# Half-height transposes, products as the stationary side and a split add in a fused RWKV and soft-MoE kernel

## The chip, the cores and the metric

The kernel runs on one core of one Trainium2 chip. The metric is the device time of one execution in microseconds (us); lower is better. The kernel before took 188.74 us as the median of three executions (191.13, 188.74 and 188.16).

In the profile PE is the matrix engine (TensorE) and PEld its weight loads, DVE the vector engine, ACT the scalar engine, POOL the general one (GpSimd), and SP the engine that issues the DMAs (SyncE). Each runs its own list of instructions in order; one that waits holds up what stands behind it on the same engine.

## The reference

Attention of the RWKV kind is computed for 4 batches, 8 heads, 768 steps and 48 features, then a soft mixture of experts on the 3072 rows that it gives.

```python
def _attn_ref(r, k, v, w, u):
    for t in range(S):
        kt, vt, rt, wt = (k[:, :, t], v[:, :, t], r[:, :, t], w[:, :, t])
        cur = np.einsum('bhd,bhe->bhde', u[None] * kt, vt)
        y[:, :, t] = np.einsum('bhd,bhde->bhe', rt, state + cur)
        state = wt[:, :, :, None] * state + np.einsum('bhd,bhe->bhde', kt, vt)

def _moe_ref(x, phi, w1, w2):           # x: 3072 x 384, 8 experts of 4 slots, F = 1024
    logits = x @ phi
    d = np.exp(logits - logits.max(0, keepdims=True))
    d /= d.sum(0, keepdims=True) + 1e-09
    slot_input = (d.T @ x).reshape(E, S_per_e, D)
    for e in range(E):
        slot_out[e] = np.maximum(slot_input[e] @ w1[e], 0.0) @ w2[e]
    c = np.exp(logits - logits.max(1, keepdims=True))
    c /= c.sum(1, keepdims=True) + 1e-09
    return c @ slot_out.reshape(n_slots, D)
```

## The kernel before, in words

**Tiling.** The 32 heads go in 16 pairs; two heads of 48 features stand on partitions 0 to 47 and 64 to 111. The 768 steps are cut into C = 6 chunks of P = 128. Within a chunk the recurrence is written as matrices. With the decays multiplied into r and k by scans, the scores k x r of a chunk, masked to earlier steps, times v give the part from within the chunk; a state carried between chunks, times r, gives the rest; and the term with u is a number per step, a = sum of u * r * k, times v. Of each batch the first three pairs of heads are loaded with all 128 partitions, whose spare rows (48 to 63 and 112 to 127) hold a third of the fourth pair each; the fourth pair's rows are gathered by DMA into tiles of their own (`k3`, `r3`, `kn3`).

**The loop.** `for it in range(NIT + 1)` is a loop of slots, unrolled, 17 of them. Slot `it` does three things for three different pairs: it prepares pair `it` (decay scans, the number a), computes pair n = it - 1 (scores, state, y), and takes pair m = it - 2 out of PSUM into x and on to the logits. What a slot contains depends on `it % 4`: slots 4, 8, 12 and 16 compute a gathered pair, whose keys need no transpose; slots 3, 7, 11 and 15 prepare no new unit, so have no `d_a`; slots 2, 6, 10 and 14 have no turn of x (`X` is false, as a third of the 384 columns of x isn't yet complete) and, from 6 on, hold steps of the softmax over the batch before.

**The order.** `tc.manual_schedule()` is on: what stands first in the loop's body goes first on each engine, and nothing is reordered. The tiles of the PSUM pool `ps_t` (four buffers), from which nearly all small PE results come, are taken in turn, so that a PE step that takes the next buffer waits for the copy that empties it. `y` has one buffer, `ps_y`.

**The steps that the change and the prediction name**, with the lines of the profile of before:

- keys, or kn: `b_kn` (matmul L298, copies L299 and L302 on ACT): transposes of five chunks of keys
- scores: `b_scores` (L313; ACT copies `at` L317; mask on POOL L318), two halves of three chunks
- `d_a` (L252; ACT copy `aT` L255) and turn of a, `d_a_turn` (L260; ACT copy `a` L263): sum over features of u * r * k, with u as the stationary operand, and its transposes. r * k is made by POOL in `d_rk` (L244)
- `b_u` (L329): keys x v for each chunk; `b_state`: the state scan `Sb` on DVE (L335) and its copy `Sn` on ACT (L338)
- x turn: `l_turn` (L384; ACT copies `xT` L386); logits, `l_part` (L401; DVE addition `lt` L410)
- `c_av` (L350): masked scores x v into y; `c_inter` (L365): r x state into the same y
- `d_av` (L284, POOL): av = v * a; `c_evac` (L375, DVE): x = y + av
- decay scans on DVE (L206 to L220), by the plans FIRST and SECOND, about half of them ahead of the state scan and half behind it; `a_pat` or `spread` (L224, ACT): the pattern for the state scan
- fillers: `keep_warm` (L793), matmuls on zeros whose result isn't used; before, only in the first two slots

## Time and profile before

| | us |
|---|---|
| median of 3 executions | 188.74 |
| the profiled execution | 189.19 |
| its span, first to last instruction | 187.4 |
| PE busy in it | 165.8 (88%) |
| DVE busy | 121.5 (65%) |
| ACT busy | 90.8 (48%) |
| POOL busy | 76.5 (41%) |
| slot 9 (76.66 to 84.19) | 7.53 |
| slot 10 (84.19 to 91.23) | 7.04 |
| slots done, start of the tail (135.2) | to 187.4: 52.2 |

Busy times of a whole span mix the loop, where DVE runs nearly all the time, with the tail of experts, where it has little to do; what a step in the loop is worth is read in a slot. In the rows of a timeline the first number is the start in us from the span's start, the second the time from the first instruction's start to the last one's end, then engine, line, operation, what it writes and reads, shapes and how many; in brackets how long the engine had been idle before and what released it. On PE the end of an instruction overlaps the start of the next, so the cost of a step there is the distance between starts. A matmul of 32-bit numbers leaves two records, a transpose one. "issue" as a releaser means that the engine waited for nothing that the profile shows.

### The profile page before, as it was taken

How to read it: one execution, taken by the hardware profiler on the slowest of the kernel's cores; microseconds unless marked ns; L12 is line 12 of the kernel's file. 1: busy time of each engine (PE TensorE's matmuls, PEld its weight loads, DVE VectorE, ACT ScalarE, POOL GpSimd, SP SyncE). 2: the span in 40 equal slices, each digit the busy share in tenths (PEclk: the TensorE clock that was granted, in tenths of full speed). 3: DMA queues.
4: the chain of work that ended last, by engine and by line, in shares of the span. 5: the costliest groups of instructions: out<-in, count | busy, mean ns of one | idle time of the engine just before them, and what ended most of it. 6: DMA issues, size and time to landing. Idle time of an engine off the chain costs nothing.

```text
span 187.4 us, 7253 instructions
## 1 busy us (share of the span) xinstructions
PE 165.8 (88%) x3000; PEld 116.6 (62%) x3000; DVE 121.5 (65%) x237; ACT 90.8 (48%) x266; POOL 76.5 (41%) x133
## 2 busy tenths in 40 slices
PE   7499979799999889999899999899789999999710
PEld 2166758677878758688777787787554324755510
DVE  5599978867897977989799889731335222033520
ACT  3054547455677726667765586784450002022430
POOL 3357286572448567445577643557004000000000
PEclk9999999969999999999999999999999999999985
DMA  5999599995779999389999259497999159907692
GB/s 148 339 396 358 116 388 328 357 406 193 230 224 366 323 397 346 75 238 319 299 368 390 53 169 285 117 330 249 418 320 415 73 167 415 417 17 294 261 385 94
DMA packets 14249, 51.93 MB, mean 277 GB/s; under 512 B 2304, under 2 KB 3200, under 8 KB 13568
## 3 DMA queue, kind: packets, MB, share of 16 engines
q1 hardware_dynamic: 14208, 51.38, 77.3%
q8 instruction: 26, 0.43, 0.9%
q14 instruction: 15, 0.12, 0.2%
HBM read 44.28 MB, written 4.72 MB: 261 GB/s over the span
## 4 chain that ended last, share of the span: by engine, by line
PE 48%; DVE 27%; DMA 7%; ACT 7%; issue 5%; POOL 1%; SPq 0%; ACTq 0%; DVEq 0%; POOLq 0%
PE ap L313 9%; DVE cst L218 6%; PE hp L536 6%; PE so L572 6%; DVE cst L206 5%; DMA rt<-in_wkr_dram 5%; PE y L365 5%; DVE Sb L335 4%; DVE ld L217 3%; PE tp L384 3%; PE op L601 3%; PE up L329 3%; ACT Sn L338 3%; PE tp L298 3%; PE sp L448 3%
## 5 line engine op out<-in xcount | busy, mean ns | idle before, releaser
L318 POOL TENSOR_SCALAR_AFFINE_SELECT at<-at 128x384 f32<-128x384 f32 x64 | 31.2, 523 | 28.7 <-ACT at L317 28.7
L317 ACT COPY at<-ap 128x384 f32<-128x384 f32 x64 | 26.4, 490 | 6.8 <-PE ap L313 5.6
L350 PE MATMUL y<-vt,at 128*64 128x48 f32 x768 | 25.5, 223 | 0.0
L350 PEld LDWEIGHTS y<-vt,at 128*64 128x64 f32 x768 | 23.7, 138 | 2.3 <-POOL at L318 1.7
L284 POOL TENSOR_TENSOR av<-vt,a 128x576 f32<-128x576 f32 x16 | 18.5, 1154 | 13.7 <-ACT a L263 13.7
L218 DVE TENSOR_TENSOR_SCAN cst<-ld,cst 128x387 f32<-128x387 f32 x24 | 23.2, 968 | 0.8
L313 PE MATMUL ap<-rt,ld 48*128 48x128 f32 x288 | 22.8, 286 | 0.7 <-issue 0.7
L206 DVE TENSOR_TENSOR_SCAN cst<-ld,cst 128x387 f32<-128x387 f32 x24 | 22.9, 953 | 0.8 <-DMA ld<-in_wkr_dram 0.6
L244 POOL TENSOR_TENSOR rk<-rt,ld 128x384 f32<-128x384 f32 x24 | 20.3, 868 | 7.3 <-DMA rt<-in_wkr_dram 4.1
L313 PEld LDWEIGHTS ap<-rt,ld 48*128 48x128 f32 x288 | 20.1, 187 | 2.2 <-issue 1.3
L335 DVE TENSOR_TENSOR_SCAN Sb<-up,pat 112x288 f32<-112x288 f32 x16 | 12.1, 753 | 11.9 <-ACT pat L224 7.4
L375 DVE TENSOR_TENSOR x<-y,av 128x576 f32<-128x576 f32 x16 | 12.1, 756 | 8.9 <-PE y L365 8.9
L338 ACT COPY Sn<-Sb 112x240 f32<-112x240 f32 x16 | 10.1, 629 | 12.2 <-DVE Sb L335 12.2
L386 ACT COPY xT<-tp 128x384 f32<-128x384 f32 x24 | 10.3, 482 | 9.0 <-PE tp L384 9.0
L217 DVE TENSOR_TENSOR ld<-ld,cst 128x387 f32<-128x387 f32 x24 | 13.0, 542 | 2.2 <-POOL rk L244 2.2
L365 PE MATMUL y<-Sn,rt 48*64 48x48 f32 x480 | 10.1, 222 | 4.6 <-ACT Sn L338 2.7
L365 PEld LDWEIGHTS y<-Sn,rt 48*64 48x64 f32 x480 | 8.4, 134 | 9.4 <-issue 3.6
L299 ACT COPY kn<-tp 128x336 f32<-128x336 f32 (+1 forms) x24 | 9.6, 401 | 8.9 <-PE tp L298 8.7
L220 DVE TENSOR_TENSOR rt<-rt,cst 128x387 f32<-128x387 f32 x24 | 13.4, 558 | 0.8
L329 PEld LDWEIGHTS up<-vt,kn 128*48 128x48 f32 x320 | 8.8, 128 | 7.0 <-issue 5.8
L572 PE MATMUL so<-wt,hT 128*32 128x208 f32 (+1 forms) x256 | 12.5, 329 | 0.0
L384 PE MATMUL tp<-ident,x 128*128 128x128 f32 x72 | 10.9, 289 | 1.0 <-DVE x L375 1.0
(130 smaller groups left out, 241.9 us busy)
## 6 DMA issues: line engine op xcount, KB each, us to landing
wt<-in_w_dram SPq DMA_DIRECT2D x24, 512.0 KB, 7.1
ld<-in_wkr_dram SPq DMA_DIRECT2D x11, 775.0 KB, 6.4
wt<-in_w_dram SPq DMA_DIRECT2D x5, 1536.0 KB, 9.0
vt<-in_v_dram SPq DMA_DIRECT2D x16, 288.0 KB, 4.9
rt<-in_wkr_dram SPq DMA_DIRECT2D x11, 387.0 KB, 5.9
wt<-in_w_dram SPq DMA_DIRECT2D x3, 832.0 KB, 6.4
out_dram<-wt SPq DMA_DIRECT2D x3, 832.0 KB, 3.9
wt<-in_w_dram SPq DMA_DIRECT2D x3, 704.0 KB, 10.1
```

Of the source, the lines that this page charges most:

```text
L206: nc.vector.tensor_tensor_scan(out=prod[:, ::-1], data0=t[:, lo + 1:lo + 1 + HALF * E1][:, ::-1], data1=one, initial=1.0, op0=ALU.mult, op ...
L217: nc.vector.tensor_tensor(out=k_, in0=k_, in1=prod, op=ALU.mult)
L218: nc.vector.tensor_tensor_scan(out=prod, data0=lds[i % NL][:, lo:lo + HALF * E1], data1=big, initial=1.0, op0=ALU.mult, op1=ALU.min)
L244: nc.gpsimd.tensor_tensor(out=rks[i % 2].rearrange("p (c e) -> p c e", e=P)[:, part], in0=queries(i)[:, part], in1=keys(i)[:, part], op=AL ...
L284: nc.gpsimd.tensor_tensor(out=av, in0=st["vv"], in1=a.broadcast_to([P, 2, C, D]), op=ALU.mult)
L313: nc.tensor.matmul(out=aps[h][:, cc, :], lhsT=kt_[rows, c * E1 + 1:(c + 1) * E1], rhs=rt_[rows, c * E1:c * E1 + P], start=True, stop=True)
L317: nc.scalar.copy(out=at, in_=aps[h])
L318: nc.gpsimd.affine_select(out=at, in_=at, pattern=[[0, 3], [1, P]], compare_op=ALU.is_gt, fill=0.0, base=0, channel_multiplier=-1)
L335: nc.vector.tensor_tensor_scan(out=Sb[0:ROWS].rearrange("p e n -> p (e n)"), data0=up[0:ROWS].rearrange("p e n -> p (e n)"), data1=(pat3 i ...
L350: nc.tensor.matmul(out=st["y"][cols, h, c * D:(c + 1) * D], lhsT=st["AT", h, hf][:, cc, cols], rhs=st["vv"][:, h, c, :], start=(c == 0), s ...
L365: nc.tensor.matmul(out=st["y"][cols, h, c * D:(c + 1) * D], lhsT=t[rows, c * E1 + 64 * th:c * E1 + 64 * th + 64], rhs=Sn[rows, c - 1, :], ...
L572: nc.tensor.matmul(out=so[32 * g:32 * g + NS, :], lhsT=hT[ft // 2][:, ft % 2, e, :], rhs=wts[E + e][:, base + ft * wd:base + (ft + 1) * wd ...
```

## The change

1. `d_a` makes r * k the stationary side, in 12 pieces of 64 steps, and moves four columns of u past each. The result has the steps on the partitions at once, so that `d_a_turn` and the copy `aT` are gone; one copy `a` on ACT is left.
2. The transposes of keys and of x are made in half-height pieces of 64 rows, which lie in two row tiles of PE: ten matmuls for five, twelve for six. The two PSUM tiles of a turn now hold the two halves by rows, not by chunks. ACT makes as many copies, cut otherwise.
3. `c_evac`, for all pairs but the last: DVE adds av to the first head of y, ACT copies the second head's y from PSUM into x, and POOL adds av to it there.
4. The order of a slot: `c_evac` first; then the scores; `d_a`; the keys' turn; `d_av`; the turn of x; and `b_u` behind it. Before: `d_av`, keys, first half of the scores, `c_evac`, second half, `d_a`, `b_u`, turn of x.
5. Fillers before `c_inter` in slots 2, 3 and 4 (six each), 8 and 12 (two each), 16 (three).

On PE, slots 9 and 10 before (`ld_99`, `ld_100`: decayed keys; `rt_103`, `rt_104`: queries):

```order
L298 MATMUL tp<-ident,ld_99 128x128 x5
L313 MATMUL ap<-rt_103,ld_99 128x128 x12
L252 MATMUL aps<-rk_134,u_sb 32x256 x3
L329 MATMUL up<-vt,kn 48x48 x10
L384 MATMUL tp<-ident,x 128x128 x6
L350 MATMUL y<-vt,at 64x48 x24
L260 MATMUL atp<-ident,aT 128x96 x2
L401 MATMUL lp<-xT,phi_sb 32x256 x3
L365 MATMUL y<-Sn,rt_103 64x48 x20
L298 MATMUL tp<-ident,ld_100 128x128 x5
L313 MATMUL ap<-rt_104,ld_100 128x128 x12
L252 MATMUL aps<-rk_133,u_sb 32x256 x3
```

and the same slots after (the steps have new lines: scores L308, `d_a` L254, keys L294, x turn L387, `b_u` L324, `c_av` L345, logits L403, `c_inter` L360):

```order
L308 MATMUL ap<-rt_103,ld_99 128x128 x12
L254 MATMUL aps<-u_sb,rk_134 64x4 x12
L294 MATMUL tp<-ident,ld_99 128x64 x10
L387 MATMUL tp<-ident,x 128x64 x12
L324 MATMUL up<-vt,kn 48x48 x10
L345 MATMUL y<-vt,at 64x48 x24
L403 MATMUL lp<-xT,phi_sb 32x256 x3
L360 MATMUL y<-Sn,rt_103 64x48 x20
L308 MATMUL ap<-rt_104,ld_100 128x128 x12
L254 MATMUL aps<-u_sb,rk_133 64x4 x12
L294 MATMUL tp<-ident,ld_100 128x64 x10
```

The scores moved ahead of the keys' turn, and `b_u` moved behind the turns of keys and of x; the two transposes of a are gone.

On ACT, slot 10 before (`kn_139` is the gathered pair's tile of keys):

```order
L299 COPY kn<-tp 128x336
L302 COPY kn_139<-tp 128x3x2x16
L299 COPY kn<-tp 128x224
L302 COPY kn_139<-tp 128x2x2x16
L317 COPY at<-ap 128x384 x4
L255 COPY aT<-aps 96x256
```

and after:

```order
L377 COPY x<-y 128x6x48
L312 COPY at<-ap 128x384 x4
L258 COPY a<-aps 128x6x4
L296 COPY kn<-tp 128x5x48 x2
L298 COPY kn_139<-tp 128x5x16 x2
```

The copy of y into x now stands ahead of the four copies of scores, and the kn copies behind them. With its waits its row reads

```order
L377 COPY x<-y 128x6x48 [waits DVE_49]
```

in each of the 15 slots; the DVE instruction that it waits for is L376, the addition for the other head of the same tile x.

The diff:

```diff
--- before.py
+++ after.py
@@ -26,6 +26,7 @@
 END_TOL = 1e-4
 N_WARM = 16
 N_WARM_2 = (5, 3, 5, 8)
+N_WAIT = {2: 6, 3: 6, 4: 6, 8: 2, 12: 2, 16: 3}
 N_FILL = (4, 3)
 N_WA = 8
 N_WB = 3
@@ -43,6 +44,7 @@
 
 NL = 4
 PART = 16
+HP = P // 2
 
 HALF = 3
 
@@ -246,22 +248,14 @@
 
     def d_a(i):
 
-        ap = ps_t.tile([TG, 2, P], F32, name="aps", tag="tp")
-        rkc = rks[i % 2].rearrange("p (c e) -> p c e", e=P)
-        for j in range(NTG):
-            nc.tensor.matmul(out=ap[32 * j:32 * j + 32], lhsT=u_sb[:, i % NU, :], rhs=rkc[:, j:C:NTG, :],
-                             start=True, stop=True)
-        parts[i] = aT = small.tile([TG, 2, P], F32, name="aT", bufs=1)
-        nc.scalar.copy(out=aT, in_=ap)
-
-    def d_a_turn(i):
-        tp = ps_t.tile([P, 2, P], F32, name="atp", tag="tp")
-        for n in range(2):
-            nc.tensor.transpose(out=tp[:, n, 0:TG], in_=parts[i][:, n, :], identity=ident[0:TG, 0:TG])
-
+        ap = ps_t.tile([P, C, 4], F32, name="aps", tag="tp")
+        for c in range(C):
+            for th in range(2):
+                nc.tensor.matmul(out=ap[HP * th:HP * th + HP, c, :],
+                                 lhsT=rks[i % 2][:, c * P + HP * th:c * P + HP * th + HP],
+                                 rhs=u_sb[:, i % NU, 0:4], start=True, stop=True)
         parts[i] = a = small.tile([P, 4, C, 1], F32, name="a", bufs=5)
-        nc.scalar.copy(out=a.rearrange("p h (n j) o -> p h n (j o)", n=2),
-                       in_=tp[:, :, 0:TG].rearrange("p n (j q) -> p q n j", q=32)[:, 0:4])
+        nc.scalar.copy(out=a.rearrange("p h c o -> p c (h o)"), in_=ap)
 
     def d_a_last(b):
         a3[b] = t = small.tile([P, 2, C, 1], F32, name="a3")
@@ -283,24 +277,25 @@
         a = a3[i // NG] if i % NG == NU else parts[unit(i)][:, 0:2]
         nc.gpsimd.tensor_tensor(out=av, in0=st["vv"], in1=a.broadcast_to([P, 2, C, D]), op=ALU.mult)
 
-    def b_kn(i, hf):
+    def b_kn(i, lo, hi):
         st = sts[i]
         if i % NG == NU:
             st["kn"] = kn3
             return
-        if hf == 0:
+        if lo == 0:
             st["kn"] = once.tile([P, C - 1, ROWS], F32, name="kn")
         kn, kv = st["kn"], keys(unit(i))
         at3 = PART * (i % NG)
-        lo, hi = ((0, 3), (3, C - 1))[hf]
-        tp = ps_t.tile([P, 3, P], F32, name="tp")
+
+        tps = [ps_t.tile([P, hi - lo, HP], F32, name="tp") for _ in range(2)]
         for c in range(lo, hi):
-            nc.tensor.transpose(out=tp[:, c - lo, :], in_=kv[:, c, :], identity=ident)
-        nc.scalar.copy(out=kn[:, lo:hi, :], in_=tp[:, 0:hi - lo, 0:ROWS])
-        src = tp[:, 0:hi - lo, :].rearrange("p c (h q) -> p c h q", h=2)[:, :, :, D:64]
-        dst = kn3[:, lo:hi, :]
-        nc.scalar.copy(out=bass.AP(tensor=dst.tensor, offset=dst.offset + at3,
-                                   ap=[dst.ap[0], dst.ap[1], [64, 2], [1, PART]]), in_=src)
+            for h in range(2):
+                rows = slice(HP * h, HP * h + HP)
+                nc.tensor.transpose(out=tps[h][:, c - lo, :], in_=kv[rows, c, :], identity=ident[rows, rows])
+        for h in range(2):
+            nc.scalar.copy(out=kn[:, lo:hi, 64 * h:64 * h + D], in_=tps[h][:, :, 0:D])
+        for h in range(2):
+            nc.scalar.copy(out=kn3[:, lo:hi, 64 * h + at3:64 * h + at3 + PART], in_=tps[h][:, :, D:HP])
 
     def b_scores(i, hf):
         st = sts[i]
@@ -372,20 +367,27 @@
         b, g = divmod(i, NG)
         if g == 0:
             xb[b] = xpool.tile([P, C, DM], F32, name="x")
-        nc.vector.tensor_tensor(
-            out=xb[b][:, :, 2 * g * D:(2 * g + 2) * D].rearrange("p c (h d) -> p h c d", h=2),
-            in0=st["y"][:, :, 0:C * D].rearrange("p h (c d) -> p h c d", c=C), in1=st["av"], op=ALU.add)
-
-    def l_turn(x, kt, pool_s, pool_t, fill=None):
+        dst = xb[b][:, :, 2 * g * D:(2 * g + 2) * D].rearrange("p c (h d) -> p h c d", h=2)
+        src = st["y"][:, :, 0:C * D].rearrange("p h (c d) -> p h c d", c=C)
+        if i == NIT - 1:
+            nc.vector.tensor_tensor(out=dst, in0=src, in1=st["av"], op=ALU.add)
+            return
+
+        nc.vector.tensor_tensor(out=dst[:, 0], in0=src[:, 0], in1=st["av"][:, 0], op=ALU.add)
+        nc.scalar.copy(out=dst[:, 1], in_=src[:, 1])
+        nc.gpsimd.tensor_tensor(out=dst[:, 1], in0=dst[:, 1], in1=st["av"][:, 1], op=ALU.add)
+
+    def l_turn(x, kt, pool_s, pool_t):
+
         xT = pool_s.tile([P, C, P], F32, name="xT")
-        for hf in range(2):
-            tp = pool_t.tile([P, 3, P], F32, name="tp")
-            for j in range(3):
-                nc.tensor.transpose(out=tp[:, j, :], in_=x[:, 3 * hf + j, kt * P:(kt + 1) * P],
-                                    identity=ident)
-            nc.scalar.copy(out=xT[:, 3 * hf:3 * hf + 3, :], in_=tp)
-            if fill and hf == 0:
-                fill()
+        tps = [pool_t.tile([P, C, HP], F32, name="tp") for _ in range(2)]
+        for c in range(C):
+            for th in range(2):
+                rows = slice(HP * th, HP * th + HP)
+                nc.tensor.transpose(out=tps[th][:, c, :], in_=x[rows, c, kt * P:(kt + 1) * P],
+                                    identity=ident[rows, rows])
+        for th in range(2):
+            nc.scalar.copy(out=xT[:, :, HP * th:HP * th + HP], in_=tps[th])
         return xT
 
     def l_seed(lt, pool_t, tag):
@@ -857,22 +859,16 @@
             d_rk(0)
             scans(0, (("G", 0), ("F", 0), ("G", 1), ("F", 1)))
             d_a(0)
-            d_a_turn(0)
             keep_warm(N_WARM_2[0], ps_t, "tp")
             d_rk(1)
         if ph == NU:
             d_a_last(it // NG)
+        if m >= 0:
+            c_evac(m)
         if B_:
-            d_av(n)
-            b_kn(n, 0)
-            if n:
-                b_kn(n, 1)
             b_scores(n, 0)
             if not n:
                 keep_warm(N_WARM_2[1], ps_t, "tp")
-                b_kn(n, 1)
-        if m >= 0:
-            c_evac(m)
         if it != 1:
             pieces_of(it, FIRST)
         if B_:
@@ -880,13 +876,16 @@
         if A and it:
             d_a(i)
         if B_:
-            b_u(n)
-        if Y:
-            s_exp(mb - 1, qs[mb - 1])
+            b_kn(n, 0, C - 1)
+            d_av(n)
         if X:
             xT = l_turn(xb[mb], mg - 1, once, ps_t)
             if mg == 1:
                 lts[mb] = small.tile([TG, 2, P], F32, name="lt", bufs=1)
+        if B_:
+            b_u(n)
+        if Y:
+            s_exp(mb - 1, qs[mb - 1])
         if B_:
             if not U_:
                 spread(pat3, k3)
@@ -910,8 +909,6 @@
             c_y(n)
             c_av(n, 0)
             c_av(n, 1)
-        if A and it:
-            d_a_turn(i)
         if X:
             l_part(mg - 1, xT, lts[mb], ps_t)
         if done is not None:
@@ -927,6 +924,8 @@
             s_slots(xb[mb - 1], mb - 1, qs[mb - 1], ps_t)
         if it == 1:
             keep_warm(N_WARM_2[3], ps_t, "tp")
+        else:
+            keep_warm(N_WAIT.get(it, 0), ps_t, "tp")
         if B_:
             c_inter(n, 0)
             c_inter(n, 1)
```

## The prediction

> **What bounds the kernel now.** I read the page first, for the span, the clock and the chain that ended last; then the windows of single slots of the loop; then the timelines of two neighbouring slots, engine by engine. From the page:
>
> ```profile
> span 187.4 us, 7253 instructions
> ...
> PE 48%; DVE 27%; DMA 7%; ACT 7%; issue 5%; POOL 1%; SPq 0%; ACTq 0%; DVEq 0%; POOLq 0%
> ```
>
> TensorE (PE) carries 48% of the chain and the vector engine (DVE) 27%. The profiled run took 189.19 us, so 1.8 us lie around its span of 187.4, and it is 0.45 above the median of 188.74: a sum made against 189.19 is lowered by 0.45 at the end. The change touches the loop only. Slots 9, 10 and 11, whose limits I cut at the first matmul of each (after length: busy us of PE, its weight loads, DVE, ACT and POOL, then granted clock and DMA):
>
> ```profile
> 76.66:84.19 7.53, 7.53 (x162) 5.97 (x157) 6.40 (x10) 5.22 (x16) 3.39 (x6) 1.00 0.61 167
> 84.19:91.23 7.04, 6.49 (x155) 5.50 (x150) 6.15 (x13) 4.92 (x17) 4.57 (x10) 1.00 0.93 331
> 91.23:99.24 8.01, 8.01 (x167) 6.18 (x162) 7.54 (x14) 5.65 (x17) 5.15 (x9) 1.00 0.97 329
> ```
>
> PE works all of slots 9 and 11, while DVE is 85% to 94% busy: two engines are close to their limit, and what ties them is the order in which each gives work to the other. PE's order in slots 9 and 10:
>
> ```profile
> 76.66 0.77 PE L298 MATMUL tp<-ident,ld 128*128 128x128 f32 x5
> 77.35 1.82 PE L313 MATMUL ap<-rt,ld 48*128 48x128 f32 x24
> 79.10 0.63 PE L252 MATMUL aps<-rk,u_sb 128*32 128x256 f32 x6
> 79.66 0.66 PE L329 MATMUL up<-vt,kn 128*48 128x48 f32 x20
> 80.25 0.87 PE L384 MATMUL tp<-ident,x 128*128 128x128 f32 x6
> 81.05 1.60 PE L350 MATMUL y<-vt,at 128*64 128x48 f32 x48
> 82.59 0.38 PE L260 MATMUL atp<-ident,aT 96*128 96x96 f32 x2
> 82.90 0.63 PE L401 MATMUL lp<-xT,phi_sb 128*32 128x256 f32 x6
> 83.46 0.80 PE L365 MATMUL y<-Sn,rt 48*64 48x48 f32 x40
> 84.19 0.77 PE L298 MATMUL tp<-ident,ld 128*128 128x128 f32 x5
> ...
> 87.25 0.66 PE L329 MATMUL up<-vt,kn 128*48 128x48 f32 x20
> ...
> 90.50 0.80 PE L365 MATMUL y<-Sn,rt 48*64 48x48 f32 x40 [0.55 <-ACT Sn L338]
> ```
>
> The cost of a step is the distance from its start to the next start: keys 0.69, scores 1.75, d_a 0.56, b_u 0.59, x turn 0.80, c_av 1.54, turn of a 0.31, logits 0.56, c_inter 0.73. And DVE and ScalarE (ACT) beside it:
>
> ```profile
> 80.43 0.76 DVE L335 TENSOR_TENSOR_SCAN Sb<-up,pat 112x288 f32<-112x288 f32 x1 [0.73 <-PE up L329]
> ...
> 84.26 0.41 DVE L410 TENSOR_TENSOR lt<-lp,lt 96x256 f32<-96x256 f32 x1
> ...
> 85.25 0.76 DVE L375 TENSOR_TENSOR x<-y,av 128x576 f32<-128x576 f32 x1
> ...
> 89.05 0.75 DVE L335 TENSOR_TENSOR_SCAN Sb<-up,pat 112x288 f32<-112x288 f32 x1
> ```
>
> ```profile
> 84.83 0.44 ACT L299 COPY kn<-tp 128x336 f32<-128x336 f32 x1 [0.83 <-PE tp L298]
> 85.17 0.24 ACT L302 COPY kn<-tp 128x96 f32<-128x96 f32 x1
> 85.30 0.36 ACT L299 COPY kn<-tp 128x224 f32<-128x224 f32 x1
> ...
> 85.91 1.63 ACT L317 COPY at<-ap 128x384 f32<-128x384 f32 x4
> ```
>
> DVE waits 0.73 for b_u in slot 9, then runs without a gap from the state scan (80.43) to the x of slot 10 (85.25), which is therefore 1.06 late against the slot's start. Today nobody needs that x soon.
>
> **The change part by part.** *Keys and x in halves.* Ten matmuls in place of five, twelve in place of six, each with 64 moving columns but still 128 stationary ones. In the c_av rows (64 stationary, 48 moving columns, one row tile) a record takes 1.54 / 48 = 32 ns; in c_inter (the same widths, but two row tiles at once) 0.73 / 40 = 18 ns. So two row tiles do share time. The nearest rows for a half are the scores, 128 stationary columns on two row tiles: 1.75 / 24 = 73 ns, which makes 10 x 73 = 0.73 for the keys and 12 x 73 = 0.88 for x. From below, at c_av's 32 ns: 0.32 and 0.38. I take no change (0.69, 0.80), near the upper end, since the width of the stationary side, which the scores share, isn't halved. Half of today's price, 0.35 and 0.40, lies near the lower end and is kept for the rivals. (The Trainium skill, "TensorEngine Tiling (Array Packing)", Theoretical Speedup, promises up to 2x for a contraction of 64 or less: by it the halves would cost just that half, and the sum below would be that of the second rival. The Trainium skill, "TensorE: Matmul & The Clock Gate", LDWEIGHTS, has a weight load grow with the columns and not with the rows, which speaks for no gain. No run so far shows a half transpose.) The number of ACT copies is unchanged (4 and 2).
>
> *d_a with r\*k stationary.* Out go 0.56 and 0.31; in come 12 matmuls, 24 records with 64 stationary columns: at c_av's 32 ns 0.77 (at 18 ns 0.43, at 73 ns 1.75). I take 0.77: -0.10. ACT loses one copy of two.
>
> *x split over three engines.* For DVE 288 elements in place of 576: between half of 0.76, which is 0.38, and the 0.41 of the lt row (256 elements) I take 0.44, a little above, so 0.32 less in each of 15 slots. ACT gains a copy of 288 elements, between the kn copies of 224 (0.36) and 336 (0.44): 0.40. GpSimd (POOL) gains an addition:
>
> ```profile
> L284 POOL TENSOR_TENSOR av<-vt,a 128x576 f32<-128x576 f32 x16 | 18.5, 1154 | 13.7 <-ACT a L263 13.7
> ```
>
> Half of 1154 ns is 0.58; POOL is busy 3.39 of 7.53 and has room. But the order of after gives that ACT copy a wait on DVE's half of the same x, and it stands ahead of the four at copies on ACT: these, the buffers that they free, and so PE, now wait for DVE.
>
> *The order.* Slot 9, counted from its start: scores 1.75, d_a 0.77, keys 0.69, x turn 0.80, so b_u begins at 4.01; now it begins at 79.66 - 76.66 = 3.00. The state scan follows b_u after 0.77 as now (80.43 - 79.66) and moves by 1.01. The 0.32 that x saves is spent waiting ahead of it, and all that DVE does behind it, to the x of slot 10, moves by 1.01 too: 85.25 + 1.01 = 86.26. PE's own slot 9 is 0.10 shorter, so slot 10 starts at 84.09 and its x comes at +2.17 instead of +1.06.
>
> Slot 10: x ends on DVE at 2.61, on ACT at 3.01; at copies from there (now at 85.91 - 84.19 = 1.72), the first done at 3.4 (1.63 / 4 each). The scores are over at 1.75 with all four buffers taken, so d_a waits until 3.4, and ends at 4.17; keys until 4.86; two kn copies (0.44 and 0.36 by the rows, overlapping) until 5.6; b_u at 5.6 instead of 3.06. From b_u to c_inter it is now 90.50 - 87.25 = 3.25, less the wait of 0.55 for Sn and the turn of a (0.31): 2.39. So c_inter comes at 8.0 and ends 0.73 later, at 8.7, against 7.04: **+1.65**. Of the wait for Sn nothing stays: the scan follows b_u by 0.77, at 6.37, as in slot 9, since DVE's other work, which lies between x and the scan today (89.05 - 85.25 = 3.80), is over at 2.17 + 3.80 - 0.32 = 5.65.
>
> Slot 11 has no d_a; b_u stands behind the x turn, 0.80 later, and DVE has 8.01 - 7.54 = 0.47 idle plus 0.32 saved, which covers it: 0. Slot 12 has gathered keys and no kn, and its scan waits for the pattern copy, which stands behind the xT copies on ACT:
>
> ```profile
> L335 DVE TENSOR_TENSOR_SCAN Sb<-up,pat 112x288 f32<-112x288 f32 x16 | 12.1, 753 | 11.9 <-ACT pat L224 7.4
> ```
>
> The x turn now comes before b_u (0.59) there, later by d_a's 0.21: 0.38 sooner, of which I take 0.3, and two fillers are paid. Their price, and the early slots:
>
> ```profile
> 18.43 1.89 PE L793 MATMUL warm<-zb 128*128 128x512 bf16 x8
> 20.25 0.80 PE L365 MATMUL y<-Sn,rt 48*64 48x48 f32 x40
> ...
> 27.74 0.80 PE L365 MATMUL y<-Sn,rt 48*64 48x48 f32 x40 [1.33 <-ACT Sn L338]
> ...
> 36.27 0.45 PE L365 MATMUL y<-Sn,rt 48*64 48x48 f32 x15 [1.21 <-issue]
> ...
> 38.67 1.07 PE L252 MATMUL aps<-rk,u_sb 128*32 128x256 f32 x6
> 39.67 1.04 PE L329 MATMUL up<-vt,kn 128*48 128x48 f32 x20
> 40.65 1.24 PE L384 MATMUL tp<-ident,x 128*128 128x128 f32 x6
> ```
>
> A filler costs (20.25 - 18.43) / 8 = 0.23. Slot 12: +0.46 - 0.3 = +0.2. A group of four slots: -0.10 + 1.65 + 0 + 0.2 = **+1.75**, and slots 5 to 16 hold three: **+5.25**. Slot 2 is built like slot 10: six fillers, 1.4, stand where 1.33 was waited for Sn, but by the same reckoning b_u comes so late that c_av ends with Sn, so they are paid, with part of the later start: +1.7. Slot 3: 1.4 less the stall of 1.21, which can pass under them: +0.2. Slot 4 lost 1.0 + 1.0 + 1.2 against 0.56 + 0.59 + 0.80 in slot 9, some 1.3 with the steps around it, to a halved clock after that stall; if the fillers keep the clock, it saves this and pays some 0.8 of its six: -0.5. Early sum **+1.4**. What keeps the clock is the loosest term: here the rows slowed down after a gap of 1.21 and not after the one of 1.33; if the fillers don't keep it, slot 4 is +0.8. (By the Trainium skill, "TensorE: Matmul & The Clock Gate", Part 1, the clock goes back to half after a window of about 3.4 us without work; fillers in gaps of 1.3 would then buy nothing, and the sum would be 1.3 higher.)
>
> No DMA is moved, and SyncE's queue is the same. PE's list grows by some 350 records on 3000, 12% (132 from the halves, 12 x 16 from d_a, 25 fillers); the chain's issue time, 5% of the span or 9.4, might grow by as much, 1.1; I take 0, since nothing tells where such a stall would fall, and keep 1.1 for the range. The sum: 189.19 + 5.25 + 1.4 = 195.84, less 0.45: **195.4**.
>
> **Rivals.** *Faster: row tiles are cheap and DVE's relief decides.* At the lower bounds (keys 0.32, x 0.38, d_a 0.43) b_u comes at 1.75 + 0.43 + 0.32 + 0.38 = 2.88, sooner than now, and slot 9 needs 7.53 - 0.37 - 0.42 - 0.44 = 6.30. x then comes at 85.13, which is 2.17 into slot 10, so that slot still pays: d_a from 3.4, b_u 4.9, end at 8.0, +0.95. But slots 11 and 12 fall to what DVE is busy, 0.32 less than the 7.54 of slot 11: 7.22 instead of 8.01, -0.79, and as much in slot 12. The group: -1.23 + 0.95 - 0.79 - 0.79 = -1.86, three times -5.6; with slot 4 at -1.3 and slots 2 and 3 at 0: 189.19 - 6.9 - 0.45 = 181.8. It decides from the point where two row tiles load their 128 columns side by side at c_av's pace. For it: c_inter's 18 ns against c_av's 32; against: the scores' 73. Chance 0.14.
>
> *About the same: the halves cost half, d_a as taken.* b_u at 3.27, slot 9 at 7.53 - 0.10 - 0.75 = 6.68; x at 85.25 + 0.27, 2.18 into slot 10; by the same steps d_a 3.4, b_u 5.2, c_inter 7.6, end 8.3, +1.3. Slots 9 and 10 together +0.45; 11 and 12 save 0.75 and 0.50 on PE less two fillers, of which DVE lets some half through, -0.4. So 0 for the group, and with the early +1.4: 190.1. Chance 0.24.
>
> *Slower still: the clock.* PE's new wait in slots 6, 10 and 14 is 3.4 - 1.75 = 1.65, longer than the 1.21 behind which the clock fell. If each costs 1.3: 195.4 + 3.9 = 199.3. It decides if a gap alone, without a burst of work ahead that differs, lowers the clock; against it stands the gap of 1.33. Chance 0.10.
>
> **How the numbers follow.** The forecast has 0.50 and the three rivals 0.48; the 0.02 left is for what I haven't thought of. A measurement here tells about 2% from no change, 185.0 to 192.5. Faster: the first rival, 0.14. Within: the second, 0.24. Slower: 0.50 + 0.10 + 0.02 = 0.62. The range takes in the second rival with d_a at its lower bound (11 x (0.77 - 0.43) = 3.7, of which I leave 1.0 to waits: 187.4), and at the top the forecast with the third rival, 199.3, or with the stalls of 1.1 and half of the scores' bound for the halves, rounded up to 199.5. Outside lie the first rival and little else.
>
> **What would show it.** The x copy on ACT in slots 6, 10 and 14 with idle time ended by DVE's x; d_a in those slots behind a wait on ACT of 1.5 or more; the state scan about 1.0 later in slots 5, 9 and 13; slot 10 near 8.7. Half transposes: 0.69 and 0.80 from start to next start. Fillers: clock 1.00 throughout slot 4. I am wrong if slot 10 stays near 7: then DVE gives x early enough, or the halves are cheap enough to hide it, and the time is 190 or less.

## The result, and the profile after

The changed kernel took 200.3 us in the median of four executions (199.1 to 202.3) against 188.6 for the kernel before (188.2 to 191.1): a ratio of 1.061, with a 95% interval of 1.053 to 1.068. Forecast were 195.4 us and a range up to 199.5. The direction was right; the time lies 0.8 us outside the range. Executions of one kernel spread (before, on one chip, 185.1 to 193.5 us at mean clocks of 0.99 to 0.94), so here and below the times are those of all executions, while a ratio with its interval compares those within 1.5% of the fastest.

The granted clock in 40 slices before, and from the page of the profile after the span, the same row and the chain by engine:

```profile
PEclk9999999969999999999999999999999999999985
```

```profile
span 198.1 us, 7949 instructions
...
PEclk9999999999985999997899699799999999999975
...
PE 63%; DVE 13%; DMA 9%; ACT 5%; issue 4%; SPq 1%; POOL 0%; ACTq 0%; DVEq 0%; POOLq 0%
```

Before, one slice of the loop was below full clock; now there are four such places. DVE's share of the chain fell from 27% to 13%, PE's rose from 48% to 63%. Slot by slot, from the start of a slot to the start of the next:

| slots | before | after | difference | forecast |
|---|---|---|---|---|
| 2, 3, 4 | 7.49, 8.19, 8.57 | 9.03, 7.90, 8.85 | +1.53 | +1.4 |
| 5, 9, 13 | 7.54, 7.53, 7.54 | 6.86, 6.85, 6.85 | -2.05 | -0.3 |
| 6, 10, 14 | 6.82, 7.04, 7.04 | 11.21, 10.05, 10.00 | +10.36 | +4.95 |
| 7, 11, 15 | 9.95, 8.01, 6.72 | 7.79, 7.79, 6.92 | -2.18 | 0 |
| 8, 12, 16 | 7.12, 7.52, 7.14 | 7.62, 9.58, 6.77 | +2.19 | +0.6 |

That is +9.85; with +0.37 ahead of slot 2 and +0.48 in the tail it makes the 10.7 by which the span grew. Windows of the slots 6 and 9 to 12 after (length, busy us of PE, its loads, DVE, ACT and POOL, then the clock and DMA):

```profile
53.99:65.20 11.21, 9.39 (x176) 8.41 (x171) 6.97 (x13) 5.27 (x18) 5.85 (x10) 0.70 0.78 258
...
80.61:87.46 6.85, 6.85 (x189) 6.02 (x184) 4.89 (x9) 5.14 (x16) 3.87 (x7) 1.00 0.61 178
87.46:97.51 10.05, 7.96 (x176) 7.13 (x170) 7.02 (x14) 5.34 (x18) 5.85 (x10) 0.83 0.78 273
97.51:105.30 7.79, 7.57 (x178) 5.78 (x172) 6.96 (x15) 5.34 (x15) 5.75 (x9) 1.00 0.97 353
105.30:114.88 9.58, 8.70 (x183) 7.24 (x177) 7.36 (x14) 4.59 (x13) 5.68 (x9) 0.82 0.39 133
```

Slots 6, 10, 12 and 14, which ran in part at half clock, grew by 2.1 to 4.4; slot 2, the only other one that grew by more than 1, did so at full clock, with a wait of 1.23 for ACT and its six fillers in it. PE's timeline of slots 9 and 10 after:

```profile
80.61 1.61 PE L308 MATMUL ap<-rt,ld 48*128 48x128 f32 x24
82.17 0.87 PE L254 MATMUL aps<-u_sb,rk 128*64 128x4 f32 x24
82.97 0.52 PE L294 MATMUL tp<-ident,ld 64*128 64x64 f32 x10
83.36 0.65 PE L387 MATMUL tp<-ident,x 64*128 64x64 f32 x12
83.94 0.85 PE L324 MATMUL up<-vt,kn 128*48 128x48 f32 x19
...
87.46 1.16 PE L308 MATMUL ap<-rt,ld 48*128 48x128 f32 x14
89.24 0.93 PE L308 MATMUL ap<-rt,ld 48*128 48x128 f32 x10 [0.63 <-DVE lt L412]
91.13 0.87 PE L254 MATMUL aps<-u_sb,rk 128*64 128x4 f32 x24 [0.96 <-ACT at L312]
91.93 0.71 PE L294 MATMUL tp<-ident,ld 64*128 64x64 f32 x10
93.14 1.21 PE L324 MATMUL up<-vt,kn 128*48 128x48 f32 x19 [0.50 <-ACT kn L296]
...
94.19 2.19 PE L345 MATMUL y<-vt,at 128*64 128x48 f32 x47
...
96.78 0.80 PE L360 MATMUL y<-Sn,rt 48*64 48x48 f32 x40
```

The rows of DVE and then of ACT that belong to them:

```profile
84.95 0.76 DVE L330 TENSOR_TENSOR_SCAN Sb<-up,pat 112x288 f32<-112x288 f32 x1 [1.59 <-PE up L324]
...
89.76 0.46 DVE L376 TENSOR_TENSOR x<-y,av 128x288 f32<-128x288 f32 x1
```

```profile
90.25 0.40 ACT L377 COPY x<-y 128x288 f32<-128x288 f32 x1 [3.06 <-DVE x L376]
90.60 1.63 ACT L312 COPY at<-ap 128x384 f32<-128x384 f32 x4
```

In slot 9 ten half transposes take 0.39 (82.97 to 83.36) where five whole ones took 0.69, and twelve take 0.58 where six took 0.80. That isn't so everywhere. In slot 11 they take 0.76 and 0.90, no less than whole ones:

```profile
99.07 0.91 PE L294 MATMUL tp<-ident,ld 64*128 64x64 f32 x10
99.83 0.97 PE L387 MATMUL tp<-ident,x 64*128 64x64 f32 x12
100.73 0.66 PE L324 MATMUL up<-vt,kn 128*48 128x48 f32 x20
```

Slots 3, 7 and 15 show the same. They have no `d_a` between the scores and the keys, and the second of a turn's two tiles waits for the next buffer of `ps_t`: its first transpose of keys starts at 99.45, when ACT's next score copy has ended (99.40).

In slot 10 ACT stands idle for 3.06 until DVE has done its half of x; the score copies start 3.14 after the slot's start, d_a 3.67 after it; PE waits three times. Behind these waits b_u takes 1.21 instead of 0.85 and c_av 2.19 instead of 1.59 in slot 9: half clock.

### The profile page after: what moved, and what is told of

Same layout as the page of the kernel before. It is cut to its first block, busy times and chain, and to the rows that moved or that the text cites. A ratio compares the mean times of both kernels' runs of the same rounds, so it can differ in the third digit from the quotient of the medians.

```text
span 198.1 us, 7949 instructions
## 1 busy us (share of the span) xinstructions
PE 173.6 (88%) x3349; PEld 125.3 (63%) x3349; DVE 117.5 (59%) x237; ACT 91.4 (46%) x269; POOL 87.5 (44%) x148
## 4 chain that ended last, share of the span: by engine, by line
PE 63%; DVE 13%; DMA 9%; ACT 5%; issue 4%; SPq 1%; POOL 0%; ACTq 0%; DVEq 0%; POOLq 0%
PE y L345 9%; PE ap L308 7%; DMA ld<-in_wkr_dram 7%; PE up L324 6%; PE so L574 6%; PE hp L538 5%; PE y L360 4%; PE aps L254 4%; PE tp L387 3%; ACT at L312 3%; PE warm L795 3%; PE op L603 3%; PE lp L403 3%; DVE cst L220 2%; DVE cst L208 2%
## 5 line engine op out<-in xcount | busy, mean ns | idle before, releaser
L378 POOL TENSOR_TENSOR x<-x,av 128x288 f32<-128x288 f32 x15 | 12.0, 800 | 47.5 <-ACT x L377 47.5
L345 PE MATMUL y<-vt,at 128*64 128x48 f32 x768 | 29.2, 236 | 0.0
L345 PEld LDWEIGHTS y<-vt,at 128*64 128x64 f32 x768 | 27.8, 153 | 0.5 <-issue 0.4
L308 PE MATMUL ap<-rt,ld 48*128 48x128 f32 x288 | 21.0, 283 | 2.5 <-DVE lt L412 1.9
L308 PEld LDWEIGHTS ap<-rt,ld 48*128 48x128 f32 x288 | 18.0, 187 | 4.6 <-DVE lt L412 2.4
L795 PE MATMUL warm<-zb 128*128 128x512 bf16 x62 | 18.0, 435 | 1.1 <-DVE cst L187 1.1
L377 ACT COPY x<-y 128x288 f32<-128x288 f32 x15 | 6.0, 400 | 24.8 <-DVE x L376 24.8
L324 PE MATMUL up<-vt,kn 128*48 128x48 f32 x320 | 14.0, 230 | 2.4 <-ACT kn L296 2.4
L254 PE MATMUL aps<-u_sb,rk 128*64 128x4 f32 x288 | 10.7, 202 | 4.9 <-ACT at L312 4.4
L324 PEld LDWEIGHTS up<-vt,kn 128*48 128x48 f32 x320 | 11.4, 140 | 4.6 <-ACT kn L296 3.3
L254 PEld LDWEIGHTS aps<-u_sb,rk 128*64 128x64 f32 x288 | 9.7, 139 | 7.3 <-ACT at L312 4.1
```

The source lines that it names most:

```text
L254: nc.tensor.matmul(out=ap[HP * th:HP * th + HP, c, :], lhsT=rks[i % 2][:, c * P + HP * th:c * P + HP * th + HP], rhs=u_sb[:, i % NU, 0:4], ...
L308: nc.tensor.matmul(out=aps[h][:, cc, :], lhsT=kt_[rows, c * E1 + 1:(c + 1) * E1], rhs=rt_[rows, c * E1:c * E1 + P], start=True, stop=True)
L324: nc.tensor.matmul(out=up[rows, :, n + 1], lhsT=st["kn"][:, n, rows], rhs=st["vv"][:, h, n, :], start=first[h], stop=(n == C - 2))
L345: nc.tensor.matmul(out=st["y"][cols, h, c * D:(c + 1) * D], lhsT=st["AT", h, hf][:, cc, cols], rhs=st["vv"][:, h, c, :], start=(c == 0), s ...
L795: nc.tensor.matmul(out=warm, lhsT=zb[:, 0, 0:P], rhs=zb.broadcast_to([P, 2, 256]), start=True, stop=True)
```

## The experiments

Times are those of four to six executions of a kernel on one chip (eleven of the one with fillers in the kernel before), beside executions of the kernel before on the same chip.

**1. Is it ACT's wait for DVE?** Two engines read the tile y and write the tile x, and the second of them in the code waits for the first: ACT for DVE here, DVE for ACT where the lines are swapped (part 4). Two edits take ACT's wait away. One swaps the two lines:

```diff
-        nc.vector.tensor_tensor(out=dst[:, 0], in0=src[:, 0], in1=st["av"][:, 0], op=ALU.add)
         nc.scalar.copy(out=dst[:, 1], in_=src[:, 1])
+        nc.vector.tensor_tensor(out=dst[:, 0], in0=src[:, 0], in1=st["av"][:, 0], op=ALU.add)
```

> The changed kernel with two lines of c_evac swapped: ACT's copy of the second head stands ahead of DVE's addition of the first, so that ACT waits for PE alone and DVE for ACT's 0.40. Theory A (the wait of ACT for DVE at the head of slots 6, 10 and 14 makes the gaps, and the gaps halve the clock): d_a in slot 10 moves from 3.67 after the slot's start to about 2.4, the clock stays full, slots 6, 10 and 14 fall from 11.2, 10.05 and 10.0 to about 8.1 each, slot 12 loses its slow stretch, 192 to 193.5 us in all. Rival B (b_u behind the turn of x, which lets DVE idle 1.6 in slots 5, 9 and 13 and be late after, is the cause; the copy is hidden anyway): d_a moves but the state scan and c_inter don't, slots 6, 10 and 14 stay above 9, over 197 us.

the other gives each head's y a tile of its own, with ACT's line first as well:

```diff
-        sts[i]["y"] = ps_y.tile([P, 2, 512], F32, name="y")
+        sts[i]["y"] = [ps_y.tile([P, 512], F32, name=f"y{h}") for h in range(2)]
```

> The changed kernel with y in two tiles of PSUM, one per head, so that neither ACT's copy nor DVE's half waits for the other; order, halves, d_a and fillers as in the change. Theory A: as with the swap of the two lines, d_a in slots 6, 10 and 14 no longer waits for DVE, 191 to 195 us, with half clock still in some windows of those slots (theory E: their work in the array is hardly more). Rival B: over 197 us.

and a third leaves all of x to DVE:

> The changed kernel with c_evac whole on DVE, as in the kernel before; ACT and POOL have no part in it. Theory A: the same relief as by the swap for ACT, but 0.3 more on DVE per slot: 192 to 195 us, slot 10 at 8.3. Rival B: over 197 us, since b_u stays late.

Measured: 192.1 to 196.0 us with the swap (no interval); 193.0 to 198.7 with two tiles (1.031 of the kernel before, 1.021 to 1.040); 191.2 to 196.5 with x whole on DVE (1.020, 1.004 to 1.037). So without the wait a third to a half of the loss is left (ratios of 1.020 and 1.031 for 1.061). Rival B, which had over 197 us in all three, falls as the whole cause. With two tiles DVE's half starts at 97.58 and ACT's copy at 97.79, though ACT's line comes first and both still write the same x: the wait came from the shared y. Slot 10 with the swapped lines, ACT and PE:

```profile
86.51 0.40 ACT L376 COPY x<-y 128x288 f32<-128x288 f32 x1 [0.16 <-PE y L360]
```

```profile
88.94 0.87 PE L254 MATMUL aps<-u_sb,rk 128*64 128x4 f32 x24
```

ACT's copy starts with the slot (86.40), and d_a comes at +2.54 (expected about 2.4). But that slot still took 9.27 with a half-clock window in it, while slot 14 of the same execution took 7.99. With two tiles slots 10 and 14 ran at full clock, 7.99 and 8.00, and slots 6, 8 and 12 at half for a part, 9.41, 9.96 (with a stall of 1.01 put down to issue) and 11.25. The wait is a half to two thirds of the story.

**2. What sets the clock?** In the trace the granted clock changes only at borders of windows 3.41 us long. I worked out for each such window what PE's array did in it: for every matmul record the rows times columns that its stationary side fills, as a share of 128 x 128, times its moving columns at 0.83 ns for 32-bit numbers (pairs of scores start 107 ns apart for 128 columns) and 0.42 for 16-bit ones (fillers of 512 columns start 216 ns apart), over 3.41 us. In the changed kernel the four windows ahead of a fall had 0.18, 0.16, 0.24 and 0.14 of the full array's work; of the others at full clock in the loop all but two (0.37 and 0.29) had 0.39 or more. To separate this from mere waiting, the same gaps were filled twice, with fillers as long but on a different part of the array. They write into a free part of the bank of b_u. In slots 6, 10 and 14 of the changed kernel (128 rows and columns of the array; the small fillers have 32 in place of 128):

```diff
             b_scores(n, 1)
+        if it in (6, 10, 14):
+            gap_fill(8, 128)
...
+        if it in (6, 10, 14):
+            gap_fill(4, 128)
         if B_:
             b_u(n)
```

> The changed kernel with twelve more fillers in each of slots 6, 10 and 14: eight behind the scores, in the wait for d_a, and four ahead of b_u, in the wait for the kn copies; each uses all 128 rows and 128 columns of the array and moves 224 columns. Theory E (the clock of a window of 3.41 us is set by the work done in the array, rows x columns x columns moved, in the window before, and a window below some 0.3 of the full array's work is followed by half clock): the window at the head of those slots rises from 0.16 to about 0.4, the three slots run at full clock and fall by 1.0 to 1.5 each: 196 to 197.5 us. Rival F (the clock is set by idle gaps, or by a budget over longer time): still half clock, no gain, 200 us or up to 1 more.

> The same twelve fillers at the same places, each with as many columns moved, but on 32 rows and 32 columns of the array only, a sixteenth of the work for the same busy time. Theory E: the window stays below 0.2, the clock falls as in the changed kernel, 199.5 to 201 us. Theory G (the share of time in which the engine is busy counts): as the full fillers, 196 to 197.5 us.

Measured: 196.2 to 202.8 us with full fillers (1.051, 1.041 to 1.060, which isn't clear of the 1.061 without them), 200.0 to 213.2 with small ones (no interval). The windows of 3.41 us in slot 10, first with full fillers, then with small ones:

```profile
91.81:95.22 3.41, 3.32 (x69) 2.63 (x68) 2.93 (x5) 3.20 (x12) 2.93 (x6) 1.00 0.93 350
95.22:98.63 3.41, 3.41 (x110) 3.19 (x106) 2.00 (x5) 2.42 (x10) 2.91 (x5) 1.00 1.02 359
```

```profile
91.46:94.88 3.42, 3.31 (x72) 2.60 (x71) 2.83 (x5) 3.21 (x13) 3.04 (x6) 1.00 0.98 349
94.88:98.29 3.41, 3.41 (x61) 3.10 (x60) 0.90 (x2) 2.01 (x7) 2.79 (x5) 0.52 0.75 256
```

PE was busy 3.32 and 3.31 us of these windows, equally much. After the one (0.44 of the array's work) the clock stayed; after the other (0.25) it fell to half. It was so in all three slots: the windows with small fillers had 0.20, 0.25 and 0.27 of the work at busy shares of 0.99, 0.97 and 0.92, and each was followed by half clock; of the windows with full fillers in these slots none was. Theory G, by which busy time counts, falls. Slots 10 and 14 with full fillers took 8.94 and 8.90, with the wait for DVE still there: full clock is worth 1.1 in each. Slot 6 took 10.87 at full clock, with an issue stall of 1.77 in it, and the clock fell in slots 2, 7 and 11, so that this execution as a whole (202.8) shows no gain.

Over slots 2 to 16 of all twenty profiled executions: of 16 windows at full clock with less than 0.25 of the array's work 15 were followed by half clock, of 70 between 0.25 and 0.37 there were 38, of 519 above 0.37 none. The share of time in which PE is busy separates them less well: of 433 windows at 0.9 or more 3 were followed by half clock (those with small fillers), of 20 below 0.6 it was 17. What decides in the middle band stays open, and my weights are only the simplest ones. The fillers changed rows and columns together. Counting rows alone leaves 103 windows that held at or below the highest that fell, columns alone 361, their product 24: the rows matter, and what the columns add isn't shown by itself. By the Trainium skill, "TensorE: Matmul & The Clock Gate", Part 1, a window of about 3.4 us without work sends the clock back to half; the length agrees (3.41), but here windows in which PE was busy 54% (1.83 of 3.41 us, slot 10 of the changed kernel) to 97% of the time did it too.

Next, the change without its own fillers:

> The changed kernel without its 25 fillers. If they are paid as I reckoned (six at 0.23 in slots 2 and 3, half of those in slot 4): 3 to 4 us less, about 196.5, provided the clock holds in slots 3 and 4. If they keep the clock: slot 4 shows rows at half speed and gets 1.3 longer, and the time stays within 1 us of 200.3.

198.6 to 199.4 us (1.054, 1.042 to 1.067). Slots 2 and 3 fell from 16.93 to 14.21; slot 4 rose from 8.85 to 10.21, with two issue stalls of 1.22 and 1.74 in it, and behind it slot 5 ran at half clock for a window and rose by 1.1. What the fillers cost and what they save cancel within what these runs can tell.

**3. The parts alone, in the old order.** The PE steps together, and one by one:

> The kernel before, in its own order, with half transposes and the new d_a alone (x whole on DVE, no fillers). In the changed kernel ten halves cost 0.39 to 0.42 where five whole cost 0.69, twelve 0.51 to 0.58 where six cost 0.80. Theory C (the PE parts are gains and the order with the split of x is what loses): PE saves 0.27 in 12 slots and 0.27 in 11, of which the slots bound by DVE keep a part: 184 to 187 us. Rival D (the pieces only move the wait, as DVE bounds the loop): 187.5 to 189.5 us.

> The kernel before with half transposes alone. By theory E each half turn does the same work in the array as a whole one in less time, and the loop, bound by DVE in slots 10 and 12, fills the rest with waiting: work per window falls a little, windows near the limit go to half clock; two to four such windows, 189 to 194 us, clock 0.94 to 0.97. If the halves don't matter for the clock: 185 to 188 us.

> The kernel before with the new d_a alone. It moves 4 columns where the old one moved 256, so its 0.8 us do next to no work in the array, where the old step's 0.56 did some. Theory E: one to three more half-clock windows, 188 to 192 us. If only waits count for the clock: within 1 us of before, as PE's time for it is the same (0.8 against 0.56 + 0.31) and ACT has one copy less.

Measured: both 193.3 to 198.5 us (1.047, 1.032 to 1.061, without the profiled execution, the fastest, which is at 1.02), halves alone 190.4 to 194.3 (1.027, 1.008 to 1.046), d_a alone 189.0 to 197.6 (no interval). Neither C nor D: not one of them is a gain, though each is shorter or as long on PE. With halves alone slot 9 takes 7.16 (before 7.53), but slot 10 takes 7.33 (before 7.04): its scores start earlier and then wait for the kn copies, and c_inter waits longer for Sn, behind a DVE that has as much to do as before; two windows with 0.36 of the array's work are followed by half clock. By the weights above a turn in halves does half the work of a whole one (each half has 64 rows and moves 64 columns, and there are twice as many), not the same, as the expectation had it. The new d_a moves 4 columns where the old one moved 256, and by the same weights does an eighth of its work. But the two windows ahead of the falls with d_a alone (0.29 and 0.27) hold no d_a: one holds a wait of 1.52 for Sn, the other one of 0.53 and an issue stall of 1.12. That d_a's little work lowers the clock isn't shown.

The split of x alone, with two tiles; then with halves; then with fillers too:

> The kernel before with x split alone (y in two tiles, so that neither engine waits for the other), whole transposes, old d_a, old order, no fillers. DVE has 0.3 less per slot, ACT 0.4 more, POOL 0.8 more; PE's work in the array is unchanged, so by theory E the clock stays as before, one or two windows at half. If DVE bounds slots 10 and 12 (c_inter waits for Sn there): 0.2 to 0.5 less in each slot of those kinds, 184 to 187.5 us where before is 188 to 189. If not: no change within 1 us.

> The one before with half transposes: 0.27 to 0.3 less of PE per turn. If PE and DVE bound the slots in turn: 182 to 186 us while the clock holds. Theory E: the halves lower the work in the array per window, so more windows at half clock than with the split alone; each costs some 1.2 to 1.7 us, so 184 to 192 us.

> The one before with full-array fillers ahead of c_inter: four in slot 2, two each in 3, 4, 6, 8, 10, 12, 14 and 16. Theory E: fewer windows at half clock than without them; faster than without them by 1 to 4 us where that run lost windows, slower by up to 2 where it lost none.

Measured: 191.7 to 194.5 (1.025, 1.012 to 1.038), 191.8 to 194.0 (1.029, 1.018 to 1.040) and 191.1 to 196.0 us (1.022, 1.011 to 1.032). With the split alone the clock is full from slot 2 to 16, and it is slower all the same. Slot 9 of it on PE and POOL, and the wait of the turn of x in the whole loop (us, times, longest):

```profile
79.75 0.87 PE L390 MATMUL tp<-ident,x 128*128 128x128 f32 x6 [0.42 <-POOL x L383]
```

```profile
77.93 0.99 POOL L318 TENSOR_SCALAR_AFFINE_SELECT at<-at 128x384 f32<-128x384 f32 x2 [1.69 <-ACT at L317]
78.89 0.80 POOL L383 TENSOR_TENSOR x<-x,av 128x288 f32<-128x288 f32 x1
79.64 1.00 POOL L318 TENSOR_SCALAR_AFFINE_SELECT at<-at 128x384 f32<-128x384 f32 x2
```

```profile
PE tp L390 <- POOL x L383: 3.2, 7, 0.5
```

The second head's x goes through ACT and then POOL, where it stands behind two masks, so the turn of x waits for POOL: slots 5, 9 and 13 take 8.03 instead of 7.54. These waits come to 3.2 in seven slots; the span grew by 3.7 (191.1 against 187.4). The relief of DVE is real (0.46 instead of 0.76), but x comes later; in the old form one engine makes it in one step.

**4. Attempts to beat both.**

> The order of the kernel before, with half transposes, the new d_a and x split with ACT's copy ahead of DVE's half; no fillers. The halves and d_a alone (x whole on DVE) left the loop bound by DVE in its undisturbed slots (c_inter waits 0.86 to 1.0 for Sn). If DVE's relief of 0.3 per slot now passes: slots 9 to 12 take 29 us in place of 30.2, and with the clock as unsteady as there 191 to 194 us; if ACT's extra copy ahead of the score copies costs as much, no gain on 193 to 197.

> As the one before, with full-array fillers ahead of c_inter, in the wait for Sn: four in slot 2, two each in slots 3, 4, 6, 8, 10, 12, 14 and 16. Theory E: they add 0.13 to 0.27 of the array's work to windows that are near the limit; fewer windows at half clock than without, 185 to 189 us. Rival F: no fewer, and 0.5 to 2 us slower than without them.

210.8 to 219.6 (1.133, 1.124 to 1.142) and 208.9 to 217.0 us (1.124, 1.112 to 1.137), the slowest of all, and against both expectations. In the old order ACT's copy of x stands behind two score copies, and by the swapped lines DVE now waits for ACT; DVE in slot 9 of the second of them:

```profile
88.09 0.46 DVE L377 TENSOR_TENSOR x<-y,av 128x288 f32<-128x288 f32 x1 [3.31 <-ACT x L376]
```

It is the wait of the changed kernel in mirror image, on the engine that makes the state. With fillers the profiled execution has 6 half-clock windows in the loop where the one without had 18, and the ratios still hardly differ, which points to the wait and not to the clock.

> The change with two y tiles, and full-array fillers in the waits that were left there: behind the first half of the scores in slots 6, 10, 14 (four) and 8, 12 (three, eight), ahead of b_u in slots 2, 6, 10, 14 (four); those ahead of c_inter in slots 2, 3 and 4 cut from six to three, four and four. Undisturbed slots of the runs before sum to 111.7 us for slots 2 to 16 against 115.2 in the kernel before. Theory E: full clock in the loop, 185 to 189 us. If half-clock windows stay: 191 to 196.

> The kernel before with fillers ahead of c_inter in slots 2 (four) and 3 (two). Its one half-clock window in the profile comes behind a window with 0.32 of the array's work, which holds the end of slot 3; two fillers add 0.13. Theory E: no half-clock window in the loop, 1.4 less in slot 4, 0.5 paid in slot 3: 0.5 to 1.5 us faster than before. Rival F: the window stays, 0.5 slower.

> The kernel before with half transposes and full-array fillers ahead of c_inter, in the wait for Sn: slots 2 (four), 3 (two), 4 (one), 6, 10 and 14 (three each). Theory E: the windows at the ends of slots 3, 6, 10 and 14 rise from 0.36 to 0.5, the loop runs at full clock, a group of four slots takes 29.2 us in place of 30.1: 184.5 to 187.5 us against 187 to 188.5 of before. If the halves lose for another reason: 188 to 192 us.

> The same idea with fillers that write into a free part of the bank of b_u, so that they take no buffer of the small results from the transposes behind them: eight short ones (224 columns) in slot 2, four in 3, two in 4, six in 6, 10 and 14, three in 11. Theory E: as the run before, 0 to 1 us faster than it, as nothing waits for their buffer.

Measured: 190.1 to 193.8 (1.028, 1.013 to 1.043), 186.9 to 196.3 (1.010, 0.9996 to 1.021), 189.7 to 195.2 (1.021, 1.014 to 1.028) and 189.4 to 196.4 us (1.013, 1.006 to 1.020). The change without its wait and with better fillers is left with half of the loss. Fillers make no measurable difference in the kernel before. With halves and fillers in a bank of their own the clock in the profiled execution is full from slot 2 to 15, and slots 9 to 12 take 7.21, 7.34, 8.02 and 7.42, in sum 29.99 against 30.10: the halves' gain on PE is spent in waiting and in fillers, though the clock holds. So for the halves theory E is not all. That DVE and the chain through both engines bound the loop, as rival D had it, fits these slots, but no run tests it by itself. No kernel here beat the one before.

## Why the prediction was wrong

**ACT's wait for DVE: right.** Forecast x at 2.17 into slot 10, score copies from 3.01, d_a at 3.4, b_u at 5.6; measured 2.30, 3.14, 3.67 and 5.68. The runs that took the wait away show it as the cause of a half to two thirds of the loss. (PE's wait of 0.63 for lt inside the scores wasn't foreseen; it cost nothing here, as PE had to wait for the score copies behind it anyway.)

**The halves: mis-sized.** I took them at the price of whole ones (0.69 and 0.80), near the scores' bound. In slots 5, 9 and 13 they cost 0.39 and 0.58, against lower bounds of 0.32 and 0.38. The scores were the wrong row: each of their records moves 128 columns, a half only 64, and the halves run in pairs, two starting within 4 ns and the next pair some 62 ns later. The Trainium skill, "TensorEngine Tiling (Array Packing)", Theoretical Speedup, promised up to 2x; measured are 1.8x for the keys and 1.4x for x in those slots. In slots 3, 7, 11 and 15 the forecast price was about right (0.76 and 0.90), by luck: the wait for a buffer sets it, which the prediction didn't have. The cheap halves made slot 9 6.85 (second rival: 6.68). They didn't bring x sooner: PE got through slot 9 sooner as well, so x is as late against slot 10, as the second rival had worked out (2.18).

**d_a: right**, 0.80 for 0.77. **x in halves: right** (DVE 0.46 for 0.44, ACT 0.40 for 0.40; POOL 0.80 for the 0.58 that I had halved).

**The clock: the step that failed.** The sum took PE to run at full clock behind its new wait and put nothing for it: 2.39 from b_u to c_inter in slot 10. It took 3.64 (93.14 to 96.78), most of it at half clock; where full fillers held the clock it took 2.72, and the slot 8.94 against the forecast 8.7. I gave half clock in slots 6, 10 and 14 a chance of 0.10 and listed it beside the cheap halves as if only one could come true. Both did. In slot 10, 3.01 over before, the runs give the parts: the wait for DVE 0.95 (8.94 with it at full clock, 7.99 without), the clock 1.11 (10.05 against 8.94), and 0.95 that is left (7.99 against 7.04), in which b_u is late and PE waits for lt and kn. Slot 6 lost two windows, slot 12 one. I argued from idle gaps, 1.21 and 1.33, as if they were what the clock reads. Read by work in the array, the window that held the 1.21 had 0.32 of it, the one with 1.33 had 0.35: both lie in the band in which either happens, so those rows could not settle it. That the new steps put less work into the array was not asked; how much of the falls is due to that, and how much to the waits, stays open.

**Early slots: right in sum** (+1.53 for +1.4), in part by luck: slots 2, 3 and 4 changed by +1.54, -0.29 and +0.28, where +1.7, +0.2 and -0.5 were forecast. The clock was 1.00 through slot 4, as forecast; without the fillers it fell behind that slot, after an issue stall of 1.74.

**Within the groups of four**, cheap halves and lost stalls gave back 4.2 in slots 5, 7, 9, 11, 13 and 15, of which 1.39 in slot 7 are two issue stalls, 0.71 and 0.68, that the changed kernel doesn't have there.

## What to carry to other kernels

Splitting one step over three engines for the sake of the busiest makes a chain of three; look first at which engine's queue each piece stands in, and at who reads the same tile, since the second reader may be made to wait for the first. A shorter step on one engine can come back as a wait in the next slot, if the engine that feeds it isn't sooner. Before thinning out TensorE's work, look at the clock row: a window in which little of the array is filled can be followed by half clock even when the engine is busy.

## What the runs showed of the hardware

In these traces the clock of TensorE changes only at borders of windows of 3.41 us, and it follows the work in the array better than the time for which the engine is busy: with PE busy 97% of a window, partly on 32 x 32 fillers, it fell; with the same busy time and 128 x 128 fillers it held. A half-clock window cost 1.1 in slot 10, which had waits of its own, and some 1.1 in slot 12: 9.58 after, 8.04 at full clock in the run without fillers, where two fillers (0.46) are less. Transposes of 64 rows in two row tiles ran in pairs some 62 ns apart in slot 9, where whole ones took 138 (0.69 for five), as long as PSUM buffers were free. And the copy from PSUM of 288 numbers per partition takes ACT 0.40 and POOL's addition of as many in SBUF 0.80, nearly twice what DVE needs (0.46) for reading PSUM and adding at once.
